# Attention loads as casting transfers on one queue, and output copies on two engines

## The chip, the cores and the metric

The kernel runs on one core of one Trainium2 chip. The metric is the time of one execution in device microseconds (us); medians of several executions are quoted, and profiles show one execution each. The span of a profile is about 2 us shorter than the time of the same execution. Engines are named as the profile names them: PE (matrix engine), PEld (its weight loads), DVE (VectorE), ACT (ScalarE), POOL (GpSimd) and SP (SyncE, which here only issues transfers).

## The reference

A decayed linear attention over 4 batches, 8 heads, 768 positions and 64 channels, followed by an expert layer with an ELU between its two products. In the kernel's terms, for chunks of 128 positions:

```python
# attention, per head, chunks of 128 (the reference uses 64; the result is the same)
out_chunk = (q k^T * decay_mask) v + (q * lam_pow) state
state     = lam_block * state + (k * rev_pow)^T v
# expert layer, x is [3072, 512]
h = x @ w_in                                  # 512 -> 2048
g = where(h > 0, h, exp(min(h, 0)) - 1)
y = g @ w_out                                 # 2048 -> 512
```

All inputs are fp32; the kernel computes in fp16 with fp32 accumulators.

## The kernel before

There are 24 chunks of attention (g = 0 to 23) and 8 token tiles of the expert layer (m = 0 to 7), three chunks to a tile. Chunks 0 to 2 are computed in a prologue. From then on one loop of 128 slots runs the expert layer, 16 slots to a tile, and the attention of the next tile is spread over the slots of this one by the function F. The parts that matter (cut):

```python
# the six chunks of batch 0: raw fp32 loads from SP, cast later on ACT and DVE
lam_p = ...                               # two loads of 64 x 4 values, every second one of lam
for c in range(NCB):
    for dst, src in zip(raw0, (q, k, v)):
        nc.sync.dma_start(out=dst[:, c], in_=src[0, :, c*L:(c+1)*L].rearrange("h p d -> p h d"))

def emit_w_load(i):                       # weights: casting loads from POOL
    nc.gpsimd.dma_start(out=wi16[i][:], in_=moe_w_in[:, f0:f1]...)
    nc.gpsimd.dma_start(out=wo16[i][:], in_=moe_w_out[f0:f1, :]...)

def att_ev(g):                            # transposed q and k out of PSUM
    nc.scalar.copy(out=qt[:], in_=pt[:, 0])
    nc.scalar.copy(out=z[0:64, :, 0, :], in_=pt[0:64, 1])
    nc.scalar.copy(out=z[64:128, :, 1, :], in_=pt[64:128, 1])

def att_SU(g, hp):                        # scores and state update of one head pair
    pu = ps.tile([128, 512], FP32, tag="psSU")       # ONE buffer
    ...three matmuls into pu...
    nc.vector.tensor_tensor(out=P[:], in0=pu[:, 0:256]..., in1=mask[...], op=ALU.mult)
    ...two state updates on nc.vector from pu...

def att_PI(g, hp):
    if hp == 0: psO[g] = ps.tile([128, NHP, 128], FP32, tag="psO")   # ONE buffer
    ...
def att_X(g):                             # frees psO
    nc.vector.tensor_tensor(out=xt[...], in0=psO.pop(g)[:], in1=qs[:], op=ALU.mult)

# at the end of a tile (its last slot but for a lag of 2)
for i in range(CPT):
    nc.vector.tensor_copy(o[:], psM[m][i][:])
    nc.sync.dma_start(out=out[t0:t0+128, :], in_=o[:])

def F(g):                                 # first slot of chunk g
    t, c = divmod(g, CPT)
    if t == 1: return 3 + 3*c
    return (t - 1)*NFT - 2 + 5*c
# T at F; SU of head pair hp at F+2+hp; PI at F+3+hp; X at F+6
```

## Time and profile before

Median 270.64 us (270.54 to 271.5) when it was predicted.

| what | before |
|---|---|
| first expert matmul (psH) starts | 31.42 us |
| from there to the end of the first tile | 47.00 us |
| later tiles, alternating | 27.94 and 27.60 us |
| last raw load used | 60.12 us |

A tile's end is read here as the start of the first psM_2 matmul of the next tile: by then all three accumulators have been copied out and PE has restarted. Those times are 35.59, 78.42, 106.36, 133.96, 161.90, 189.50, 217.44 and 243.84.

First, lines of the page of the kernel before: the span, PE's busy share, then the busy tenths of PE and of the transfer engines (DMA) in 40 slices of 6.7 us each, and the shares of the chain of work that ended last.

```profile
span 268.1 us, 4675 instructions
PE 224.0 (84%) x1632; PEld 134.2 (50%) x1632; DVE 192.2 (72%) x461; ACT 159.8 (60%) x351; POOL 73.4 (27%) x111
...
PE   0166678585989998999899989999899989998991
...
DMA  0999999999998479567956894793300030003003
...
PE 63%; SPq 15%; DVE 8%; DMA 7%; issue 4%; ACT 1%; DVEq 0%; ACTq 0%
```

PE's row stays at 8 or less through slice 10 (67 us), and its 9s follow one another only from slice 13 (80 us) on. The DMA row is at 9, its highest digit, from slice 2 to slice 12: transfers are under way all through the start. SPq in the chain is SP's issuing.

The table of stretches of the kernel before (busy us and instructions of each engine, granted clock, DMA share, rate):

```profile
core 0: us, PE busy (x) PEld busy (x) DVE busy (x) ACT busy (x) POOL busy (x), PEclk, DMA share, GB/s
20.00:30.00 10.00, 6.44 (x51) 5.37 (x52) 9.50 (x27) 2.28 (x5) 5.05 (x7) 1.00 1.48 175
...
80.00:100.00 20.00, 20.00 (x157) 12.30 (x155) 17.96 (x45) 14.54 (x33) 8.65 (x11) 1.00 0.68 47
```

From 20 to 30 us DVE is busy 9.50 of 10 us: it paces the prologue. From 80 us PE is busy throughout. (The DMA share in this view adds up the recorded times of all packets over 16 engines; above 1, as in 1.48, it means that packets overlapped on an engine.)

The timeline of the kernel before (start us, duration us, engine, line, operation, out<-in; in brackets idle time just before and what ended it):

```profile
1.24 1.36 SPq L64 DMA_DIRECT2D lam_p<-in_lam_dram  x2
...
3.92 4.70 SPq L74 DMA_DIRECT2D raw_v<-in_v_dram  x1
...
31.42 1.44 PE L312 MATMUL psH_381<-xt_265,wi_0_104 128*128 128x384 f16 x4 [0.78 <-DVE xt_265 L298]
...
60.12 0.43 DVE L190 CAST v_5_153<-raw_v 128x512 f16<-128x512 f32 x1 [2.45 <-DMA raw_v<-in_v_dram]
...
104.42 0.69 DVE L345 COPY osb_0_1308<-psM_0_909 128x512 f32<-128x512 f32 x1
105.03 0.68 DVE L345 COPY osb_1_1311<-psM_1_910 128x512 f32<-128x512 f32 x1
...
105.16 0.38 PE L338 MATMUL psM_0_1345<-wo_0_109,g_1277 128*128 128x512 f16 x1 [0.86 <-DVE osb_0_1308 L345]
105.62 0.68 DVE L345 COPY osb_2_1314<-psM_2_911 128x512 f32<-128x512 f32 x1
...
105.76 0.38 PE L338 MATMUL psM_1_1346<-wo_0_109,g_1277 128*128 128x512 f16 x1 [0.22 <-DVE osb_1_1311 L345]
...
106.36 0.38 PE L338 MATMUL psM_2_1347<-wo_0_109,g_1277 128*128 128x512 f16 x1 [0.22 <-DVE osb_2_1314 L345]
```

The third raw load's issue keeps SP for 4.70 us. The last raw_v is cast at 60.12, and DVE waited 2.45 us for it. At the tile end (104 to 107 us) three DVE copies run one after the other, 0.60 apart, and each restart of PE waits for one of them.

### The profile page before, as it was taken

To read this page: it belongs to the slowest core of one execution; us is meant where nothing else is said; L and a number is where in the kernel's file an instruction comes from. 1 tells how busy PE (TensorE), PEld (TensorE's weight loads), DVE (VectorE), ACT (ScalarE), POOL (GpSimd) and SP (SyncE) were. 2 spreads that over 40 slices of the span, in tenths; PEclk is the share of its full clock that TensorE was granted. 3 is DMA by queue.
4 is the path that set the end of the run, shared out by engine and by line. 5 is a ranking of instruction groups with operands and counts; after the bars stand their busy time and mean duration, and the time that the engine had idled before them with its cause. 6 is when DMAs were issued, how large, how long until landed. Compare 5 with 4: busy or idle time off the path is not lost.

```text
span 268.1 us, 4675 instructions
## 1 busy us (share of the span) xinstructions
PE 224.0 (84%) x1632; PEld 134.2 (50%) x1632; DVE 192.2 (72%) x461; ACT 159.8 (60%) x351; POOL 73.4 (27%) x111
## 2 busy tenths in 40 slices
PE   0166678585989998999899989999899989998991
PEld 0045434243555664666466655665466546553550
DVE  1259646437699979977789979867999799655443
ACT  2673078362647764776577576757666756764660
POOL 8195414225524430433242333232000000000000
PEclk9999999889999999999999999999999999999999
DMA  0999999999998479567956894793300030003003
GB/s 1 205 210 183 174 180 177 196 176 111 63 172 55 31 49 118 77 43 48 86 111 44 57 59 129 50 60 22 119 2 0 0 120 0 2 0 120 0 2 119
DMA packets 84104, 22.60 MB, mean 84 GB/s; under 512 B 76400, under 2 KB 81008, under 8 KB 84080
## 3 DMA queue, kind: packets, MB, share of 16 engines
q0 software_dynamic: 61216, 11.28, 51.1%
q1 hardware_dynamic: 22864, 11.02, 17.6%
q8 instruction: 13, 0.21, 0.3%
q14 instruction: 11, 0.09, 0.1%
HBM read 27.27 MB, written 6.29 MB: 125 GB/s over the span
## 4 chain that ended last, share of the span: by engine, by line
PE 63%; SPq 15%; DVE 8%; DMA 7%; issue 4%; ACT 1%; DVEq 0%; ACTq 0%
SPq L74 14%; DMA raw_v<-in_v_dram 7%; PE psM_2_2205 L338 1%; PE psM_2_3057 L338 1%; PE psM_2_2627 L338 1%; PE psM_2_1769 L338 1%; PE psM_2_911 L338 1%; PE psM_2_1347 L338 1%; PE psM_0_1767 L338 1%; PE psM_0_1345 L338 1%; PE psM_0_2625 L338 1%; PE psM_0_2203 L338 1%; PE psM_0_909 L338 1%; PE psM_1_1346 L338 1%; PE psM_1_2204 L338 1%
## 5 line engine op out<-in xcount | busy, mean ns | idle before, releaser
L312 PEld LDWEIGHTS <-wi_3_107 128*128 128x128 f16 x128 | 12.7, 100 | 14.5 <-DMA wi_3_107<-in_moe_w_in_dram 2.5
L312 PEld LDWEIGHTS <-wi_2_106 128*128 128x128 f16 x128 | 12.5, 98 | 11.7
L312 PEld LDWEIGHTS <-wi_4_108 128*128 128x128 f16 x128 | 12.5, 98 | 11.7
L218 PE MATMUL psT_187<-ident_118,qn_182 128*128 128x128 f16 x4 | 0.6, 308 | 12.6 <-ACT qn_182 L188 12.6
L312 PEld LDWEIGHTS <-wi_1_105 128*128 128x128 f16 x64 | 6.4, 100 | 8.9 <-issue 4.2
L242 PEld LDWEIGHTS <-kz_154 128*128 128x128 f16 x96 | 8.3, 105 | 4.9 <-POOL kd_200 L201 1.5
L181 POOL DMA_DIRECT2D v_3_151<-in_v_dram x6 | 4.5, 753 | 22.4 <-PE psO_2149 L289 8.7
L312 PEld LDWEIGHTS <-wi_0_104 128*128 128x128 f16 x64 | 6.5, 103 | 7.5 <-issue 2.0
L242 PEld LDWEIGHTS <-kz_155 128*128 128x128 f16 x96 | 8.0, 101 | 3.5 <-issue 1.4
L181 POOL DMA_DIRECT2D v_0_148<-in_v_dram x6 | 4.5, 757 | 15.6 <-PE psO_1715 L282 8.4
L181 POOL DMA_DIRECT2D v_1_149<-in_v_dram x6 | 4.5, 750 | 13.5 <-PE psO_1003 L289 5.0
L181 POOL DMA_DIRECT2D v_4_152<-in_v_dram x6 | 4.5, 755 | 12.4 <-PE psO_1441 L289 5.0
L181 POOL DMA_DIRECT2D v_5_153<-in_v_dram x6 | 4.5, 756 | 11.7 <-PE psO_2431 L289 4.3
L181 POOL DMA_DIRECT2D v_2_150<-in_v_dram x6 | 4.5, 757 | 9.3 <-PE psO_1140 L289 4.6
L141 DVE TENSOR_TENSOR mask<-causT,dn 128x1024 f32<-128x1024 f32 x1 | 1.2, 1224 | 7.8 <-ACT dn L130 7.8
L218 PEld LDWEIGHTS <-qn_182 128*128 128x128 f16 x4 | 0.3, 130 | 12.6 <-ACT qn_182 L188 12.6
L317 ACT ACTIVATE e_386<-psH_381 128x384 f32<-128x384 f32 x1 | 0.5, 492 | 8.6 <-PE psH_381 L312 8.6
L282 PEld LDWEIGHTS <-v_2_150 128*128 128x128 f16 x32 | 3.4, 106 | 3.4 <-issue 1.9
L282 PEld LDWEIGHTS <-v_4_152 128*128 128x128 f16 x32 | 3.2, 99 | 3.7 <-issue 1.8
L282 PEld LDWEIGHTS <-v_1_149 128*128 128x128 f16 x32 | 3.4, 108 | 2.6 <-issue 1.0
L282 PEld LDWEIGHTS <-v_5_153 128*128 128x128 f16 x32 | 3.1, 98 | 2.8 <-issue 0.9
L282 PEld LDWEIGHTS <-v_0_148 128*128 128x128 f16 x32 | 3.2, 108 | 2.3 <-issue 0.6
(1917 smaller groups left out, 863.6 us busy)
## 6 DMA issues: line engine op xcount, KB each, us to landing
raw_q<-in_q_dram SPq DMA_DIRECT2D x6, 256.0 KB, 8.8
raw_k<-in_k_dram SPq DMA_DIRECT2D x6, 256.0 KB, 9.7
raw_v<-in_v_dram SPq DMA_DIRECT2D x6, 256.0 KB, 10.0
wi_2_106<-in_moe_w_in_dram POOLq DMA_DIRECT2D x1, 512.0 KB, 15.4
wo_2_111<-in_moe_w_out_dram POOLq DMA_DIRECT2D x1, 512.0 KB, 17.7
wi_3_107<-in_moe_w_in_dram POOLq DMA_DIRECT2D x1, 512.0 KB, 17.6
wo_3_112<-in_moe_w_out_dram POOLq DMA_DIRECT2D x1, 512.0 KB, 20.2
wi_4_108<-in_moe_w_in_dram POOLq DMA_DIRECT2D x1, 512.0 KB, 19.8
```

The source lines that it names most:

```text
L74: nc.sync.dma_start(out=dst[:, c], in_=src[0, :, c * L : (c + 1) * L].rearrange("h p d -> p h d"),)
L141: nc.vector.tensor_tensor(out=mask[:], in0=causT[:].unsqueeze(1).broadcast_to([128, H, 128]), in1=dn[:].unsqueeze(2).broadcast_to([128, H, ...
L181: nc.gpsimd.dma_start(out=vz[:, :, 2 * hh, :], in_=v[b, hh::2, rows].rearrange("h p d -> p h d"))
L218: nc.tensor.transpose(pt[:, 0, hp, :], in_=qn[:, 2 * hp : 2 * hp + 2, :], identity=ident16[:])
L242: nc.tensor.matmul(pu[:, hh * 128 : (hh + 1) * 128], lhsT=z[:, hp, hh, :], rhs=qt[:, hp, :], start=True, stop=True,)
L282: nc.tensor.matmul(po[:, hp, :], lhsT=vz[:, hp, hh : hh + 2, :], rhs=P[:, hh, :], start=(hh == 0), stop=(hh == 1 and cb == 0), skip_group_ ...
L312: nc.tensor.matmul(pH[:], lhsT=wi[:, kk, j * 128 : (j + 1) * 128], rhs=xt[m][:, kk, :], start=(kk == 0), stop=(kk == NHP - 1),)
L317: nc.scalar.activation(e[:], pH[:], AF.Exp)
L338: nc.tensor.matmul(psM[m][i][:], lhsT=g[:, i * 128 : (i + 1) * 128], rhs=wo16[wof[n][0]][:, wof[n][1], :], start=(n == 0), stop=(n == NFT ...
```

## The change

Its intent: load every chunk's q, k and v with casting transfers from POOL, all on one queue with the weights and in the order of need; lay v out with a zero block beside every head, so that one load fills it; and share the copying of outputs between DVE and ACT. Cut to its core:

```diff
-    lam_p = ...two loads of every second lam...
-    raw0 = [...fp32 tiles...]; for c in range(NCB): ...nc.sync.dma_start(raw...)...
+    v2 = [cpool.tile([128, 2 * H, 64], FP16, ...) for i in range(NB)]
+    def emit_load(g, which=(0, 1, 2)):
+        jobs = ((qn[:], q), (kn[:], k), (vz[:, 0::2, :], v))
+        for dst, src in [jobs[i] for i in which]:
+            nc.gpsimd.dma_start(out=dst, in_=src[b, :, rows].rearrange("h p d -> p h d"))
+    emit_load(0, (0, 1))
...
-    nc.scalar.activation(loglam_p[:], lam_p[:], AF.Ln)
+    for hh in range(2): nc.vector.tensor_copy(loglam_p[r, :], loglam[r, hh::2])
...
+    emit_load(0, (2,)); emit_load(1); emit_load(2)
...
-        nc.gpsimd.memset(...)      # zeros in kz, v3 and st: 18 memsets
+        nc.vector.memset(...)      # the same for kz, v2 and st, after the mask
...
-        nc.scalar.copy(out=qt[:], in_=pt[:, 0])
+        if g < CPT: nc.vector.tensor_copy(qt[:], pt[:, 0])
+        else:       nc.scalar.copy(out=qt[:], in_=pt[:, 0])
...
-                    nc.vector.tensor_copy(new[r, r], u)     # state of a first chunk
+                    nc.scalar.copy(new[r, r], u)
...
-                nc.vector.tensor_copy(o[:], psM[m][i][:])
+                if i == 1: nc.vector.tensor_copy(o[:], psM[m][i][:])
+                else:      nc.scalar.copy(o[:], psM[m][i][:])
...
+    emit_w_load(0); emit_w_load(1); emit_load(3); emit_w_load(2); emit_load(4)
+    emit_w_load(3); emit_load(5); emit_w_load(4)
```

More of the change, by code (lines that the diff above doesn't have):

```diff
@@ L51 @@
     wpool = ctx.enter_context(tc.tile_pool(name="w", bufs=1))
-    raw = ctx.enter_context(tc.tile_pool(name="raw", bufs=1))
     nat = ctx.enter_context(tc.tile_pool(name="nat", bufs=6))
@@ L60 @@
     nc.sync.dma_start(out=lam_b[:], in_=lam.unsqueeze(0).broadcast_to([128, H]))
-    lam_p = cpool.tile([128, NHP], FP32, name="lam_p")
-    for hh in range(2):
-        nc.sync.dma_start(
-            out=lam_p[hh * 64 : (hh + 1) * 64, :],
-            in_=lam[hh::2].unsqueeze(0).broadcast_to([64, NHP]),
-        )
-    raw0 = [
-        raw.tile([128, NCB, H, 64], FP32, name=f"raw_{n}", tag=f"raw_{n}") for n in "qkv"
-    ]
-    for c in range(NCB):
-        for dst, src in zip(raw0, (q, k, v)):
-            nc.sync.dma_start(
-                out=dst[:, c],
-                in_=src[0, :, c * L : (c + 1) * L].rearrange("h p d -> p h d"),
-            )
+    NB = 6
+    v2 = [cpool.tile([128, 2 * H, 64], FP16, name=f"v2_{i}") for i in range(NB)]
+    nats = {}
+    def emit_load(g, which=(0, 1, 2)):
+        b, c = divmod(g, NCB)
+        rows = slice(c * L, (c + 1) * L)
+        if 0 in which:
+            qn = nat.tile([128, H, 64], FP16, tag="qn", name=f"qn{g}")
+            kn = nat.tile([128, H, 64], FP16, tag="kn", name=f"kn{g}")
+            nats[g] = (qn, kn, v2[g % NB])
+        qn, kn, vz = nats[g]
+        jobs = ((qn[:], q), (kn[:], k), (vz[:, 0::2, :], v))
+        for dst, src in [jobs[i] for i in which]:
+            nc.gpsimd.dma_start(out=dst, in_=src[b, :, rows].rearrange("h p d -> p h d"))
+    emit_load(0, (0, 1))
     WG = [2, 2, 4, 4, 4]
@@ L104 @@
     loglam_p = cpool.tile([128, NHP], FP32, name="loglam_p")
-    nc.scalar.activation(loglam_p[:], lam_p[:], AF.Ln)
+    for hh in range(2):
+        r = slice(hh * 64, (hh + 1) * 64)
+        nc.vector.tensor_copy(loglam_p[r, :], loglam[r, hh::2])
     ident16 = cpool.tile([128, 128], FP16, name="ident16")
@@ L122 @@
     nc.gpsimd.iota(iota_r[:], pattern=[[1, 128]], base=0, channel_multiplier=0)
+    emit_load(0, (2,))
+    emit_load(1)
+    emit_load(2)
     pos = cpool.tile([128, 2], FP32, name="pos")
@@ L146 @@
     )
-    NB = 6
-    v3 = [cpool.tile([128, NHP, 3, 64], FP16, name=f"v3_{i}") for i in range(NB)]
     kz = [cpool.tile([128, NHP, 2, 128], FP16, name=f"kz_{i}") for i in range(2)]
@@ L156 @@
     for i in range(2):
-        nc.gpsimd.memset(kz[i][64:128, :, 0, :], 0.0)
-        nc.gpsimd.memset(kz[i][0:64, :, 1, :], 0.0)
+        nc.vector.memset(kz[i][64:128, :, 0, :], 0.0)
+        nc.vector.memset(kz[i][0:64, :, 1, :], 0.0)
     for i in range(NB):
-        nc.gpsimd.memset(v3[i][:, :, 1, :], 0.0)
+        nc.vector.memset(v2[i][:, 1::2, :], 0.0)
     for hp in range(NHP):
         for i in range(2):
-            nc.gpsimd.memset(st[hp][i][:], 0.0)
-    nats = {}
-    def nat_tiles(g):
-        qn = nat.tile([128, H, 64], FP16, tag="qn", name=f"qn{g}")
-        kn = nat.tile([128, H, 64], FP16, tag="kn", name=f"kn{g}")
-        nats[g] = (qn, kn, v3[g % NB])
-        return nats[g]
-    def emit_load(g):
-        b, c = divmod(g, NCB)
-        qn, kn, vz = nat_tiles(g)
-        rows = slice(c * L, (c + 1) * L)
-        nc.gpsimd.dma_start(out=qn[:], in_=q[b, :, rows].rearrange("h p d -> p h d"))
-        nc.gpsimd.dma_start(out=kn[:], in_=k[b, :, rows].rearrange("h p d -> p h d"))
-        for hh in range(2):
-            nc.gpsimd.dma_start(
-                out=vz[:, :, 2 * hh, :], in_=v[b, hh::2, rows].rearrange("h p d -> p h d")
-            )
-    def emit_cast_first(c):
-        qf, kf, vf = raw0
-        qn, kn, vz = nat_tiles(c)
-        nc.scalar.copy(qn[:], qf[:, c])
-        nc.scalar.copy(kn[:], kf[:, c])
-        nc.vector.tensor_copy(
-            vz[:, :, 0::2, :], vf[:, c].rearrange("p (g t) d -> p g t d", t=2)
-        )
+            nc.vector.memset(st[hp][i][:], 0.0)
     kds = {}
@@ L199, in att_kd @@
         kd = asb.tile([128, H, 64], FP16, tag="kd", name=f"kd{g}", bufs=2)
-        eng = nc.gpsimd if g == 0 else nc.vector
-        eng.tensor_tensor(
+        nc.vector.tensor_tensor(
             out=kd[:], in0=nats[g][1][:],
@@ L229, in att_ev @@
         z = kz[g % 2]
-        nc.scalar.copy(out=qt[:], in_=pt[:, 0])
-        nc.scalar.copy(out=z[0:64, :, 0, :], in_=pt[0:64, 1])
-        nc.scalar.copy(out=z[64:128, :, 1, :], in_=pt[64:128, 1])
+        if g < CPT:
+            nc.vector.tensor_copy(qt[:], pt[:, 0])
+        else:
+            nc.scalar.copy(out=qt[:], in_=pt[:, 0])
+        for hh in range(2):
+            r = slice(hh * 64, (hh + 1) * 64)
+            nc.scalar.copy(out=z[r, :, hh, :], in_=pt[r, 1])
         qT[g] = (qt, z)
@@ L250, in att_SU @@
                 lhsT=kds[g][:, 2 * hp : 2 * hp + 2, :],
-                rhs=vz[:, hp, 0::2, :], start=True, stop=True,
+                rhs=vz[:, 4 * hp : 4 * hp + 3 : 2, :], start=True, stop=True,
             )
@@ L283, in att_PI @@
                 po[:, hp, :],
-                lhsT=vz[:, hp, hh : hh + 2, :],
+                lhsT=vz[:, 4 * hp + hh : 4 * hp + hh + 2, :],
                 rhs=P[:, hh, :], start=(hh == 0), stop=(hh == 1 and cb == 0),
@@ L344, in mm2 @@
                 o = msb.tile([128, DM], FP32, tag="osb", bufs=4, name=f"osb{m}_{i}")
-                nc.vector.tensor_copy(o[:], psM[m][i][:])
+                if i == 1:
+                    nc.vector.tensor_copy(o[:], psM[m][i][:])
+                else:
+                    nc.scalar.copy(o[:], psM[m][i][:])
                 t0 = m * MT + i * 128
@@ L364 @@
         f = F(g)
-        evs.append((f, lambda g=g: (emit_cast_first(g) if g < NCB else None, att_T(g), att_ev(g), att_kd(g))))
+        evs.append((f, lambda g=g: (att_T(g), att_ev(g), att_kd(g))))
         for hp in range(NHP):
@@ L372 @@
         at(s, fn)
-    loads = [(-1, lambda: emit_w_load(0)), (-1, lambda: emit_w_load(1))]
-    loads += [(4 * i - 4, lambda i=i: emit_w_load(i)) for i in range(2, len(WG))]
-    for g in range(NCB, NG):
-        loads.append((F(g) - 12, lambda g=g: emit_load(g)))
-    loads.sort(key=lambda x: x[0])
-    for g in range(CPT):
-        emit_cast_first(g)
-        if g == 1:
-            loads.pop(0)[1]()
-        if g == 2:
-            loads.pop(0)[1]()
+    emit_w_load(0)
+    emit_w_load(1)
+    emit_load(3)
+    emit_w_load(2)
+    emit_load(4)
+    emit_w_load(3)
+    emit_load(5)
+    emit_w_load(4)
+    loads = [(F(g) - 12, lambda g=g: emit_load(g)) for g in range(NCB, NG)]
+    for g in range(CPT):
         att_T(g)
```

## The prediction

> **What bounds the kernel now.**
>
> 1. Prologue, 0 to 31.4 us: PE idles; the first expert matmul (psH_381) starts at 31.42 (timeline). VectorE paces it: in 20 to 30 us it is busy 9.50 of 10 us (windows table).
> 2. First token tile, 31 to 78 us: loads. The chain of waits runs through SyncE's load issues (14%) and raw_v's DMA (7%). In the trace's packet records for 48 to 54 us the two queues advance one for one: about 310 weight packets (1024 B) and 312 raw packets (256 B) per 2 us. The Trainium skill, "DMA: Bandwidth & Descriptors", section Queues, rings and completion order, says each engine alternates between queues packet by packet; the trace agrees. So small raw loads move at the pace of large weight packets, 40 GB/s, and the last raw_v lands at 60.1. The first tile's closing-to-closing time (psM_2's restart, 35.59 to 78.42) is 42.8 us; later tiles take 27.54 to 27.94 (mean 27.80).
> 3. Steady state, 80 to 262 us: PE, chain of waits nearly all psH matmuls. By the pure-matmul slot time of 1.297 us a tile would need about 25.8; the other 2 us sit mostly at the tile end, where PE waits for three serial VectorE copies (osb, spaced 0.60): at 104.1 to 106.57 it loses about 1.8 us.
>
> **What changes, with costs.**
> - Removed: 12 ScalarE casts (0.62 each), 6 VectorE casts (0.43 to 0.77), the 256-byte queue, and the lam_p load, whose landing at 8.77 held up the exponentials (near 5 after).
> - Moved to VectorE, before its first attention work: 18 memsets, v's zeros doubled. The skill, "VectorE: DVE Perf Modes", section Zero memsets, gives one cycle per element; my estimate from it is 0.55 for 512 elements, about 6.5 us in all. No trace shows one yet: my largest unknown. Also three qT copies (estimate 0.5) and kd(0) (0.68).
> - One queue, in order. Between 60 and 62 us casting loads alone moved 1216 packets per us, so a 1024-packet load needs 0.84 us of transfer and about 0.9 of POOL issue; the nine first loads land by about 13 us (landing 3.7 to 3.9 after issue). Weights (4.2 MB written, 155 GB/s) and the next nine loads then land by about 45, ahead of use in every slot.
> - Steady state: two of three osb copies and each first chunk's state copies go to ScalarE; VectorE drops to about 22.5 us per tile.
>
> **Critical path.** VectorE free at about 13, then about 15 us of the three prologue chunks: first expert matmul at 27.5 (gain 4). First tile: 42.8 to about 30 (gain 13; attention is denser there and VectorE may bind). Six later boundaries: gain 1.2 each, period about 26.5 (gain 7). Final copies: gain 0.6. Sum about 25 us of 270.64.
>
> **Prediction: 245.5 us, 80% range 240 to 252. Chances: faster by over 2% 0.97, within 2% 0.02, slower 0.01.**
>
> **Signs.** First psH matmul at 25 to 30 us; no PE wait on a DMA after it; no second cold-clock stretch (now 52.2 to 55.6); psM_2 restarts 26 to 27 us apart; last weight landed before 48 us; VectorE memsets 5 to 7 us in all.
>
> **What would make it wrong.** Memsets costing 2 us or 10; POOL's issue slowed while VectorE works, so chunks 1 and 2 come late; the first tile's dense attention making VectorE bind, keeping it at 33 or more; ScalarE's copies delaying the exponentials and moving the boundary bubble rather than filling it.

## More of the kernel before

The eight PSUM banks are all in use: psT, psSU and psO have one each, psM three, psH two.

## The result and the profile after

Median 250.68 us (250.40 to 250.93, 4 runs) against 270.86 us (270.54 to 271.5, 4 runs) for the kernel before in the same rounds. Ratio 0.9252, 95% interval 0.9231 to 0.9273. A ratio is the mean time of one kernel's runs over that of the other's of the same rounds, so it is not quite the ratio of the medians quoted.

The page of the changed kernel, the same lines (slices of 6.2 us):

```profile
span 248.7 us, 4595 instructions
PE 220.5 (89%) x1632; PEld 133.8 (54%) x1632; DVE 178.7 (72%) x431; ACT 164.7 (66%) x383; POOL 72.1 (29%) x92
...
PE   0186797869999989999999989999999999999991
...
DMA  6999999999995596499589769563000020003003
...
PE 66%; DMA 8%; ACT 8%; DVE 7%; issue 4%; POOL 4%; ACTq 0%; DVEq 0%; POOLq 0%
```

PE's 9s follow one another from slice 10 (56 us) on, in place of 80 us. The DMA row is again at 9 from slice 2 to slice 12: the transfers are as busy as before, yet they stop PE far less. SPq is gone from the chain.

The stretches of the changed kernel:

```profile
core 0: us, PE busy (x) PEld busy (x) DVE busy (x) ACT busy (x) POOL busy (x), PEclk, DMA share, GB/s
...
40.00:58.00 18.00, 13.98 (x124) 9.05 (x123) 12.96 (x34) 9.07 (x21) 10.85 (x13) 1.00 2.07 151
...
80.00:100.00 20.00, 19.35 (x153) 11.84 (x151) 17.33 (x44) 13.91 (x33) 5.26 (x6) 1.00 0.83 86
```

Between 40 and 58 us PE is busy 13.98 of 18 us. Something in the first tile still stops it; the experiments show what.

The start of the changed kernel in the timeline:

```profile
7.62 0.27 DVE L162 MEMSET kz_143<- 64x256 uint32 x1
...
11.11 0.11 DVE L168 MEMSET st_1_152<- 128x64 uint32 x1
11.14 0.35 DVE L207 COPY qT_205<-psT_196 128x512 f16<-128x512 f16 x1
...
11.53 1.19 ACT L212 COPY kz_143<-psT_196 64x512 f16<-64x512 f16 x2 [3.82 <-DVE qT_205 L207]
...
21.00 0.42 DVE L207 COPY qT_310<-psT_301 128x512 f16<-128x512 f16 x1
...
21.52 1.19 ACT L212 COPY kz_143<-psT_301 64x512 f16<-64x512 f16 x2 [4.82 <-DVE qT_310 L207]
...
27.78 1.44 PE L292 MATMUL psH_376<-xt_267,wi_0_87 128*128 128x384 f16 x4 [0.78 <-DMA wo_2_94<-in_moe_w_out_dram]
```

The memsets run from 7.62 to 11.2 us, just before the first qT copy on DVE. ACT's kz copy begins only when DVE's qT copy has ended, after 3.82 and 4.82 us of idling. The first psH matmul starts at 27.78. Its bracket names a load of wo_2, a tile that this matmul does not read; DVE's xt_267, which it reads, ended at 27.73. The label is of the kind that is looked at under c_space4.

Where the 19.4 us of the two spans (268.1 and 248.7) came from. Each row is a difference of two times in the timelines.

| stage | before | after | gain | gain predicted |
|---|---|---|---|---|
| start to first expert matmul | 31.42 | 27.78 | 3.6 | 3.9 |
| from there to the end of the first tile | 47.00 | 37.08 | 9.9 | 13 |
| the six tiles after it | 165.42 | 159.94 | 5.5 | 7 |
| the last tile and the final copies | 24.26 | 23.90 | 0.4 | 0.6 |

The gains came in the stages predicted, but the sum was 5 us too large, most of it in the first tile. The prediction gave the delay of that tile one reason, the loads, and named its dense attention only as a risk.

### The profile page after: what moved, and what is told of

Read it like the earlier page. It is cut to its first block, busy times and chain, and to the rows that moved or that the text cites. A ratio compares the mean times of both kernels' runs of the same rounds, so it can differ in the third digit from the quotient of the medians.

```text
span 248.7 us, 4595 instructions
## 1 busy us (share of the span) xinstructions
PE 220.5 (89%) x1632; PEld 133.8 (54%) x1632; DVE 178.7 (72%) x431; ACT 164.7 (66%) x383; POOL 72.1 (29%) x92
## 4 chain that ended last, share of the span: by engine, by line
PE 66%; DMA 8%; ACT 8%; DVE 7%; issue 4%; POOL 4%; ACTq 0%; DVEq 0%; POOLq 0%
DMA wo_2_94<-in_moe_w_out_dram 4%; DMA wi_0_87<-in_moe_w_in_dram 3%; PE psM_1_2165 L318 1%; PE psM_1_1313 L318 1%; ACT kz_144 L212 1%; PE psM_2_2166 L318 1%; PE psM_2_1314 L318 1%; PE psM_1_3012 L318 1%; PE psM_0_1312 L318 1%; PE psM_2_3013 L318 1%; PE psM_0_2164 L318 1%; DMA kn_991<-in_k_dram 1%; PE psM_0_3011 L318 1%; PE psM_0_3371 L318 1%; PE psM_0_879 L318 1%
## 5 line engine op out<-in xcount | busy, mean ns | idle before, releaser
L77 POOL DMA_DIRECT2D v_3_80<-in_v_dram x4 | 3.6, 906 | 16.2 <-PE psO_1259 L269 8.1
L77 POOL DMA_DIRECT2D v_0_77<-in_v_dram x4 | 3.5, 880 | 15.8 <-PE psO_1680 L262 7.7
L77 POOL DMA_DIRECT2D v_5_82<-in_v_dram x4 | 3.5, 878 | 15.3 <-PE psO_2391 L269 5.0
L77 POOL DMA_DIRECT2D v_4_81<-in_v_dram x4 | 3.5, 878 | 13.1 <-PE psO_2260 L269 5.6
L77 POOL DMA_DIRECT2D v_1_78<-in_v_dram x4 | 3.6, 889 | 11.6 <-PE psO_1825 L269 5.9
L77 POOL DMA_DIRECT2D v_2_79<-in_v_dram x4 | 3.6, 896 | 10.7 <-PE psT_2046 L198 5.5
L222 PE MATMUL psSU_0_211<-qT_205,kz_143 128*128 128x128 f16 x2 | 0.6, 288 | 5.5 <-ACT kz_143 L212 5.5
L194 PE MATMUL psT_196<-ident_102,qn_83 128*128 128x128 f16 x4 | 0.6, 308 | 4.8 <-DMA qn_83<-in_q_dram 4.8
L212 ACT COPY kz_143<-psT_301 64x512 f16<-64x512 f16 x2 | 1.2, 580 | 4.8 <-DVE qT_310 L207 4.8
```

The lines of the kernel that those rows point to most:

```text
L77: nc.gpsimd.dma_start(out=dst, in_=src[b, :, rows].rearrange("h p d -> p h d"))
L194: nc.tensor.transpose(pt[:, 0, hp, :], in_=qn[:, 2 * hp : 2 * hp + 2, :], identity=ident16[:])
L212: nc.scalar.copy(out=z[r, :, hh, :], in_=pt[r, 1])
L222: nc.tensor.matmul(pu[:, hh * 128 : (hh + 1) * 128], lhsT=z[:, hp, hh, :], rhs=qt[:, hp, :], start=True, stop=True,)
```

## The experiments

Twelve kernels ran, all correct. "Start" is the first psH matmul; "first tile" goes from there to the tile's end. This second number varies by up to 1 us between traces of kernels that do not differ there, and most of that is the moment at which the matrix clock rises, since the first slots run at half clock. (The Trainium skill, "TensorE: Matmul & The Clock Gate", section What's actually happening, has PE start at half clock and rise after about 3.4 us of work, and calls the moment variable. The traces agree roughly: in the changed kernel the grant is full from 31.9 us, 4.1 us after the start; over all runs this took 2.6 to 6.0 us.) Medians of different rounds are compared with care: the kernel before itself took 270.86 to 272.11 us in them, and j_late_loads, whose edit turned out to move nothing, lies 0.8 us below the changed kernel. Differences of about 1 us in the median are therefore read from the traces, not from the medians.

| kernel | start | first tile | later periods | median us | ratio |
|---|---|---|---|---|---|
| before | 31.42 | 47.00 | 27.94 / 27.60 | 270.86 | 1 |
| changed | 27.78 | 37.08 | 27.39 / 26.17 | 250.68 | 0.9252 |
| a_osb_dve | 27.57 | 37.31 | 28.36 / 27.06 | 256.82 | 0.9455 |
| b_evac_only | 32.47 | 44.71 | 27.41 / 26.17 | 264.57 | 0.9727 |
| c_space4 | 27.66 | 32.80 | 27.39 / 26.17 | 245.96 | 0.9054 |
| h_osb_act | 27.67 | 37.84 | 26.62 / 26.66 | 249.56 | 0.9179 |
| d_memset_first | 24.27 | 37.94 | 27.39 / 26.17 | 247.13 | 0.9084 |
| e_no_lam_p | 29.25 | 42.88 | 27.94 / 27.60 | 263.58 | 0.9696 |
| f_small_w | 31.51 | 44.85 | 27.94 / 27.60 | 266.81 | 0.9821 |
| j_late_loads | 27.78 | 36.79 | 27.38 / 26.17 | 249.89 | 0.9197 |
| g_qT_act | 26.27 | 38.01 | 27.39 / 26.17 | 249.48 | 0.9187 |
| k_evac_no_lam_p | 30.51 | 41.05 | 27.40 / 26.16 | 257.37 | 0.9488 |
| i_comb2 | 24.32 | 32.85 | 26.62 / 26.16 | 240.42 | 0.8854 |
| l_comb3 | 23.55 | 32.71 | 26.62 / 26.17 | 239.49 | 0.8821 |

### Undo the evacuation (a_osb_dve), and do it alone (b_evac_only)

```diff
 # a_osb_dve, on the changed kernel
-                if i == 1: nc.vector.tensor_copy(...)
-                else:      nc.scalar.copy(...)
+                nc.vector.tensor_copy(o[:], psM[m][i][:])
 # b_evac_only, on the kernel before
+                if i == 1: nc.vector.tensor_copy(...) else: nc.scalar.copy(...)
-                    nc.vector.tensor_copy(new[r, r], u)
+                    nc.scalar.copy(new[r, r], u)
```

> The changed kernel with all three output copies of a tile put back on VectorE (the state copies of first chunks stay on ScalarE). My theory: the tile-end wait of PE for three serial VectorE copies (0.60 apart) returns in full; tile periods go from 27.39/26.17 back to about 27.8/27.4, over seven tile ends, and the whole to 255 to 258 us. Rival: the shorter periods come from VectorE's relief over the whole tile (fewer copies, no load casts), not from the wait at the tile end; then putting 1.2 us per tile back on VectorE, which has about 4 us of room per tile, costs under 2 us and the whole stays below 252.5.

> The kernel before with only the evacuation part of the change: output copies 0 and 2 and the state copies of first chunks on ScalarE, loads untouched. If the two parts act in different stages, this gains about what the tile ends are worth, 5 to 6 us: 264 to 266 us, with the first tile still at 42 to 43 us between restarts of psM_2 and later periods of 26 to 27.4. If the parts depend on each other (the evacuation only helps once the loads no longer stall PE), it gains under 2 us.

Undone, the kernel takes 256.82 us, 6.1 more, and every period grows by 0.9 to 1.0. Done alone on the kernel before, it gains about 7.3 us and gives the same periods as the whole change, 27.41 and 26.17. So the later periods belong to this part alone, and it does not need the loads' part. Two details were not expected. Alone, it also shortened the first tile by 2.3 us. And the start came 1.05 us later: there the state copies of chunk 0 were the only part of the edit that ran before the first expert matmul. In its trace ACT's first cast for chunk 1 comes at 18.41 in place of 15.47, behind eight state copies that begin at 16.65, and PE waits 2.02 us for it.

### Chunks four slots apart in the first tile (c_space4), and later loads (j_late_loads)

What stops PE between 40 and 58 us of the changed kernel? The chain of waits gives this answer (start us, duration us, what):

```profile
50.62 3.24 DMA kn_991<-in_k_dram
53.85 0.27 PE psO_706 L262 x2
```

The timeline around that moment, and around two more stops:

```profile
43.37 0.27 PE L222 MATMUL psSU_0_576<-qT_515,kz_143 128*128 128x128 f16 x2 [1.27 <-DVE st_0_151 L248]
...
45.27 0.69 DVE L278 TENSOR_TENSOR xt_601<-psO_494,qs 128x512 f16<-128x512 f32 x1
...
46.02 0.27 PE L262 MATMUL psO_603<-pp_0_580,v_4_81 128*128 128x128 f16 x2 [0.86 <-DVE xt_601 L278]
...
50.62 0.88 POOL L77 DMA_DIRECT2D kn_991<-in_k_dram  x1
...
53.11 0.69 DVE L278 TENSOR_TENSOR xt_601<-psO_603,qs 128x512 f16<-128x512 f32 x1 [0.57 <-PE psO_603 L269]
...
53.85 0.27 PE L262 MATMUL psO_706<-pp_0_681,v_5_82 128*128 128x128 f16 x2 [0.78 <-DMA kn_991<-in_k_dram]
```

The load of kn_991 was issued at 50.62 and belongs to a chunk that is not computed for many slots. The instruction that it is said to release, psO_706, writes a buffer that DVE's xt_601 had to read out first, and xt_601 ran from 53.11 to 53.80. The label is wrong; which event a wait belongs to is inferred by time. The other brackets name the same kind of release: psSU waits for DVE's last read of it (st, 1.27 us), psO for xt (0.86 us).

The kernel before has the same stops in its first tile, 1.11 and 1.29 us for psSU and twice 0.78 for psO, among its waits for loads and casts. The first of them:

```profile
52.10 0.35 PE L242 MATMUL psSU_0_597<-qT_533,kz_154 128*128 128x128 f16 x2 [1.11 <-DVE st_0_162 L268]
```

These stops come from the schedule. A chunk needs SU at slots F+2 to F+5, PI at F+3 to F+6 and X at F+6. In the first tile chunks start three slots apart, so the next chunk's first SU falls in the same slot as this one's last, and its first PI in the same slot as this one's X. Both pairs share a single PSUM buffer, so PE stands still until DVE has worked off its queue. Later tiles use five slots and never meet.

```diff
 # c_space4, on the changed kernel
         if t == 1:
-            return 3 + 3 * c
+            return 1 + 4 * c
 # j_late_loads, on the changed kernel
-    loads = [(F(g) - 12, lambda g=g: emit_load(g)) for g in range(NCB, NG)]
+    loads = [(F(g) - 6, lambda g=g: emit_load(g)) for g in range(NCB, NG)]
```

> The changed kernel with one number changed: the chunks of the first tile's attention stage start at slots 1, 5, 9 in place of 3, 6, 9. My theory: the first tile takes 32.7 us in place of 26 to 27.4 because with three slots between chunks two chunks meet in one slot, and share single PSUM buffers: PE waits 1.27 and 1.10 us for psSU, and 0.86 and 0.78 for psO, with VectorE's queue behind it. With four slots between they never meet: first tile 28 to 30 us, the whole 246.5 to 248.5. Rival, which the chain of waits names: PE waits there for the transfer of k (3.24 us put down to a load of kn): then bringing chunks 3 and 4 forward helps nothing, and the whole stays at 250.7 or gets longer.

> The changed kernel with the loads of chunks 6 and later issued 6 slots ahead of use in place of 12. The chain of waits puts 3.24 us of the first tile down to a load of kn (chunk 8 or 9), at a time when the DMA engines move loads that nobody needs for many slots. My theory: that is a mislabel (the real release is VectorE's xt copy), so taking these loads out of 44 to 54 us changes nothing: 250.7 within 0.5. Rival: the loads' traffic does hold up the first tile: 1.5 to 3 us faster.

With four slots between chunks the kernel takes 245.96 us, 4.7 less and a little better than expected, and the first tile loses 4.3 us. The time from restart to restart is then 27.63, close to that of later tiles, and of the waits for psSU and psO in that tile 0.18 us is left. The stretch in which PE was busy 13.98 of 18 us:

```profile
core 0: us, PE busy (x) PEld busy (x) DVE busy (x) ACT busy (x) POOL busy (x), PEclk, DMA share, GB/s
40.00:58.00 18.00, 17.68 (x144) 10.86 (x142) 14.52 (x34) 12.42 (x29) 12.70 (x15) 1.00 2.21 157
```

PE is now busy 17.68 of 18, with the transfers just as busy (DMA share 2.21 here, 2.07 before the edit). That answers the rival: the same traffic, and PE hardly waits.

j_late_loads was meant to answer it too, but its edit did not do what the text above says. The same row of its trace:

```profile
40.00:58.00 18.00, 13.99 (x122) 8.91 (x120) 12.95 (x33) 9.08 (x21) 10.10 (x12) 1.00 2.10 152
```

The loads are still there. Chunk 6's first load was issued at 41.68 us in place of 42.46, and between 44 and 54 us 155 GB/s moved in both kernels. POOL's program has nothing but loads at this point, so the slot in which one is emitted does not hold it back; it is issued as soon as POOL gets to it and its buffers are free. The first tile stayed as it was (32.67 from restart to restart, 32.68 without the edit), which says nothing about the traffic. The total, 249.89 us, is 0.8 below the changed kernel, outside the 0.5 expected, and shows how far medians of different rounds differ when nothing has changed.

So the spacing was the cause and the transfers were not. That the single buffers are the way in which the spacing acts is read from the waits; no run gave psSU or psO a second buffer.

### All output copies on ACT (h_osb_act)

The tile end that costs most in the changed kernel, in its timeline:

```profile
89.85 0.59 ACT L328 COPY osb_0_1276<-psM_0_879 128x512 f32<-128x512 f32 x1
...
90.32 0.62 ACT L328 COPY osb_2_1282<-psM_2_881 128x512 f32<-128x512 f32 x1
...
91.01 0.38 PE L318 MATMUL psM_0_1312<-wo_0_92,g_1245 128*128 128x512 f16 x1
...
91.29 0.69 DVE L326 COPY osb_1_1279<-psM_1_880 128x512 f32<-128x512 f32 x1
...
92.03 0.38 PE L318 MATMUL psM_1_1313<-wo_0_92,g_1245 128*128 128x512 f16 x1 [0.65 <-DVE osb_1_1279 L326]
...
92.25 0.38 PE L318 MATMUL psM_2_1314<-wo_0_92,g_1245 128*128 128x512 f16 x1
```

ACT's two copies are done by 90.9, but the middle one waits in DVE's queue until 91.29, so psM_1 restarts at 92.03, 0.65 us late.

```diff
-                if i == 1: nc.vector.tensor_copy(...)
-                else:      nc.scalar.copy(...)
+                nc.scalar.copy(o[:], psM[m][i][:])
```

> The changed kernel with all three output copies of a tile on ScalarE. My theory: what is left of the bubble (PE waits about 0.65 to 0.8 us for the middle copy, which stands behind VectorE's backlog at every second tile end) goes, periods become 26.1 to 26.5 throughout, the whole 247 to 249. Rival: three ScalarE copies in a row (1.7 us) hold up the next exponentials and the bubble moves there: no gain, 250 to 252.

The periods became flat, 26.62 and 26.66; the total fell by about 1 us only. At the odd tile ends, where DVE has a backlog, three ACT copies are better by 0.77 us. At the even ones, where DVE is free, they are worse by 0.49. In the timeline of this kernel, at an even tile end, the next exponential stands behind the three copies:

```profile
117.17 1.56 ACT L325 COPY osb<-psM 128x512 f32<-128x512 f32 x3
...
117.81 1.35 PE L318 MATMUL psM<-wo,g 128*128 128x512 f16 x3
...
118.61 0.52 ACT L297 ACTIVATE e<-psH 128x384 f32<-128x384 f32 x1
```

PE's three restarts spread over 1.35 us here, where those of the odd end before it took 0.84, and the exponential starts 1.44 us after the first copy, where it takes 0.96 at the same end of the changed kernel. Both theories were half right: the total (249.56 us) lies between their ranges. The best version below uses each form where it is better.

### The memsets first (d_memset_first)

```diff
     v2 = [cpool.tile(...)]
+    kz = ...; st = ...          # tiles and all 18 nc.vector.memset(...) moved here,
                                 # ahead of DVE's first other work
```

> The changed kernel with VectorE's 18 memsets moved to the head of its program, where it idles for its first 3.6 us. My theory: the memsets (7.62 to 11.14 us, 3.5 us in all) stand on the critical path between the mask and the first chunk's qT copy; moved, the first expert matmul starts 2.5 to 3.2 us earlier (24.6 to 25.3 in place of 27.79) and the whole is 247.4 to 248.4. Rival: the loads of chunks 1 and 2 (landing about 11 and 13.6 us) or the first tile's wait for weights pace the start: gain under 1 us, or given back in the first tile.

The first expert matmul came at 24.27, 3.5 us earlier, and the kernel took 247.13 us, 3.55 less; both are slightly better than expected. (The span of the profiled execution gained only 2.7; its clock rose 5.9 us after the start in place of 4.1.) The 18 memsets were practically wholly on the critical path, though they need no input and DVE was idle for the first 3.6 us. They cost 3.6 us in all, not the 6.5 of the prediction. The Trainium skill, "VectorE: DVE Perf Modes", section Zero memsets, gives one cycle per element, and also says that a zero memset can be issued over 4-byte words, halving the elements of fp16. The trace shows that this was done: 256 uint32 elements for 512 fp16 ones, 0.27 us each. The prediction used the rule and overlooked the second half of it.

### The qT copies back on ACT (g_qT_act)

ACT's kz copies and DVE's qT copy only read the same psT tile, yet one engine waits for the other. The Trainium skill, "PSUM — Partial Sum Buffer", section Terms, lists two engines on one bank and partition group at once as an error, "reads against reads included". That is a reason for such a wait, which therefore can't simply be dropped; no run here shows the error.

```diff
-        if g < CPT: nc.vector.tensor_copy(qt[:], pt[:, 0])
-        else:       nc.scalar.copy(out=qt[:], in_=pt[:, 0])
+        nc.scalar.copy(out=qt[:], in_=pt[:, 0])
```

> The changed kernel with the first three chunks' qT copies put back on ScalarE. In the changed kernel ScalarE's kz copies begin only after VectorE's qT copy of the same psT tile has ended, and so stand behind VectorE's queue (3.82 us of ScalarE idling in chunk 0, 4.82 in chunk 2), while VectorE then waits 1.11, 0.54 and 0.43 us for the products that need kz. Theory: the move of qT to VectorE cost more than it saved; undone, the first expert matmul starts 0.8 to 1.8 us earlier (26.0 to 27.0) and the whole is 249.0 to 250.0. Rival: ScalarE needs 0.5 us more per chunk in series, and the start stays at 27.8 or gets later.

The start came at 26.27, 1.5 us earlier, within the range expected. In the timeline ACT's copies of chunk 0 now run while DVE still fills zeros (kz at 8.09 in place of 11.53):

```profile
7.63 0.56 ACT L206 COPY qT<-psT 128x512 f16<-128x512 f16 x1
...
8.09 1.18 ACT L209 COPY kz<-psT 64x512 f16<-64x512 f16 x2
```

So moving qT to DVE was a loss as the change stands. Little of the gain can be seen in the total: 249.48 us, 1.2 less. The interval of its ratio (0.9160 to 0.9215) lies just below that of the changed kernel (0.9231 to 0.9273), but inside that of j_late_loads (0.9151 to 0.9243), which does the same work as the changed kernel. In its trace the first tile is 0.9 us longer: full clock came 6.0 us after the start, in place of 4.1.

### The kernel before without lam_p (e_no_lam_p)

```diff
-    lam_p = cpool.tile([128, NHP], FP32, name="lam_p")
-    for hh in range(2): nc.sync.dma_start(out=lam_p[...], in_=lam[hh::2]...)
-    nc.scalar.activation(loglam_p[:], lam_p[:], AF.Ln)
+    for hh in range(2): nc.vector.tensor_copy(loglam_p[r, :], loglam[r, hh::2])
```

> The kernel before without the two small lam_p loads (4-byte pieces, first in the loading queue); the same values are copied from lam_b, as the change does. My theory: prologue starts earlier (the raw loads' packets begin near 3 us in place of 6.7, the exponentials near 5 in place of 9) and the first expert matmul comes 2 to 4 us sooner, but the last raw_v still lands near 57 to 60 us, since the shared queues pace it, so most of the gain is given back in the first tile: 267.5 to 270.5 us. Rival: the start is worth its full 3 us to the end: 267.5 or less.

It gained 7.7 us (263.58 against 271.24). The theory's range was missed; the rival's (267.5 or less) holds, but for more than its reason: the start moved only 2.2 us. The issues of SP in this kernel's timeline, to be set beside those of the kernel before:

```profile
1.24 0.42 SPq L68 DMA_DIRECT2D raw_q<-in_q_dram  x1
...
2.33 1.30 SPq L68 DMA_DIRECT2D raw_v<-in_v_dram  x1
...
3.67 0.89 SPq L68 DMA_DIRECT2D raw_q<-in_q_dram  x1
```

SP is no longer held for 4.70 us, and the packet records agree. Counted there:

| | before | without lam_p |
|---|---|---|
| 4-byte packets on SP's queue up to 9.2 us | 581 | 99 |
| first 256-byte raw packet | 7.10 us | 2.32 us |
| raw packets begun by 10 us | 2334 | 6348 |
| first weight packet | 16.1 us | 14.5 us |
| last raw packet | 59.6 us | 48.0 us |

Two loads of 1 KB each, cut into 4-byte pieces, stood ahead of the raw loads and held them up by 4.8 us. The Trainium skill, "DMA: Bandwidth & Descriptors", section Rules for kernel authors, says that a strided last dimension lowers to one descriptor per element; the traces agree: SP's queue moved 544 fewer 4-byte packets in all (688 in place of 1232) for two loads of 512 values together. Why was the gain larger than the 2.2 us at the start? Until weights join in, the raw loads have the transfer engines to themselves and move at 214 to 239 GB/s (counted in steps of 2 us). Afterwards they share, and in the kernel before they move at 33 to 111. So 4.8 us more of undisturbed time brought the last raw packet forward by 11.6 us, and the first tile, which waits for it, lost 4.1 us.

### Small weight packets in the kernel before (f_small_w)

```diff
-        nc.gpsimd.dma_start(out=wi16[i][:], in_=moe_w_in[:, f0:f1]...)
-        nc.gpsimd.dma_start(out=wo16[i][:], in_=moe_w_out[f0:f1, :]...)
+        for j in range(WG[i]):   # blocks of 128 columns
+            nc.gpsimd.dma_start(out=wi16[i][:, :, j*128:(j+1)*128], in_=...)
+        for j in range(4):
+            nc.gpsimd.dma_start(out=wo16[i][:, :, j*128:(j+1)*128], in_=...)
```

> The kernel before with each weight load cut into column blocks of 128, so that its packets write 256 B in place of 1024 (or 512); same bytes, same order, more packets and more issues on POOL. My theory of the first tile before: the two queues advance one packet each in turn, so the 256-byte raw packets move at 40 GB/s only because each waits for a 1024-byte weight packet. Then raw packets in the shared stretch advance at 80 GB/s or more, the last raw_v lands before 50 us in place of 60.1, and the first tile shortens by 4 us or more (unless late weights take its place). Rival: the raw loads are held by the sheer number of packets or bytes, or by SyncE's issue: then more packets make it worse, and the last raw_v lands at 60 or later.

With weight packets of 256 bytes the raw loads moved at 85 to 130 GB/s between 32 and 40 us, where those of the kernel before had 39 to 46 between 44 and 54 us beside 1024-byte packets. The last raw packet landed at 45.1 in place of 59.6, though nothing was changed about the raw loads. That fits the alternation of the skill's section Queues, rings and completion order, which the prediction rests on. The counts are about one for one here too: 3344 raw and 2957 weight packets from 32 to 40 us. (The page's packet holds several descriptors; whether a turn is one of the trace's packets or several, the counts don't tell.) The kernel gained 4.4 us, with an interval of 1.3% to 2.3%, though the weights, now slower, arrived until 61.2 us (59.5 before). One part of the expectation failed: the first tile was to lose 4 us or more and lost 2.1 (44.85 in place of 47.00), although the last raw load came 14.5 us earlier. Late weights took little of it back (PE waited 0.34 us for one); the clock, full 5.8 us after the start in place of 3.7, took an estimated 1 us. So the slow raw loads were only a part of what made the old first tile long; the stops at psSU and psO are in this trace as well (1.11, 0.86, 1.11 and 0.78 us).

### The two small parts together (k_evac_no_lam_p)

The edits of b_evac_only and e_no_lam_p together on the kernel before.

> The kernel before with two small parts of the change and none of its casting loads: no lam_p loads, and the evacuation on two engines. If the two single gains (7.7 and 7.3 us) lie in different stages they add: 255.5 to 257 us; what the casting loads on one queue are worth beyond that is then the rest to 250.7, about 5 to 6 us, a quarter of the whole gain. If they overlap in the first tile (both shortened it), 258 or more.

257.37 us, 14.1 less than the kernel before (271.51): nearly the sum of 7.3 and 7.7, a little outside the range expected. So about 70% of the change's 20.2 us come from not loading lam_p by elements and from the output and state copies. All the rest, casting loads on one queue and the moves that go with them, is worth about 6.5 us: 2.7 at the start (30.51 against 27.78) and 4.0 in the first tile (41.05 against 37.08). No run separates the parts of this rest.

### Everything that helped (i_comb2, l_comb3)

```diff
 # i_comb2 on the changed kernel: c_space4, d_memset_first, g_qT_act, and
-                if i == 1:
+                if i == 1 and m % 2 == 0:
                     nc.vector.tensor_copy(o[:], psM[m][i][:])
 # l_comb3 on i_comb2: qT of chunks 0 and 1 back on DVE
+        if g < 2: nc.vector.tensor_copy(qt[:], pt[:, 0])
+        else:     nc.scalar.copy(out=qt[:], in_=pt[:, 0])
```

> Everything that helped, together: chunk spacing 4 in the first tile, VectorE's memsets at its head, qT of the first chunks on ScalarE, and the middle output copy on ScalarE too at every second tile end (the odd tiles, where VectorE has a backlog). If the gains lie in different stages they add: 4.7 + 3.5 + 2.2 + 1.3 off 250.7, 238.5 to 240.5 us; first expert matmul at 22.5 to 23.5, first tile 26.5 to 28, later periods 26.1 to 26.7 throughout. Rival: the earlier start runs into the loads of chunks 1 to 3 or the first weights, and 2 us or more are given back: 241.5 or more.

> The best version so far (240.42 us) with the qT copies of chunks 0 and 1 back on VectorE and only chunk 2's on ScalarE. Moving the memsets alone gave a first expert matmul at 24.27, and qT on ScalarE added nothing to it (24.32), though alone it was worth 1.5 us. My reading: with the memsets gone VectorE is the freer engine in chunks 0 and 1 (it waits 1.64 and 1.02 us there for products that need ScalarE's kz), and only in chunk 2, where ScalarE idles 2.36 us, is qT better on ScalarE. Then the first expert matmul comes at 23.4 to 24.0 and the whole is 239.4 to 240.2. Rival: the start is now set by VectorE's total work whatever engine copies qT; then 24.3 to 24.8 and 240.4 or more.

i_comb2 took 240.42 us. The gains of the first tile and of the tile ends added; those at the start did not. The memsets alone gave 24.27, with qT on ACT as well 24.32. Both edits attacked the same wait: once DVE was free early, ACT became the engine that chunks 0 and 1 waited for. l_comb3 follows from that and copies qT on the freer engine in each chunk; its start is 23.55, and its time 239.49 us, ratio 0.8821 (0.8791 to 0.8850). It is the best version, 4.5% below the changed kernel.

## Why the prediction was right, and where its sizes were off

- **The range and the direction.** 250.68 us lies inside 240 to 252, near its upper end. The estimate of 245.5 was 5.2 us too low.
- **The prologue (27.5 predicted, 27.78 measured) was right by two errors that cancelled.** The memsets were priced at 6.5 us and took 3.6. The three chunks after DVE became free were given about 15 us and took 16.6 (11.14 to 27.78); the wait of ACT's kz copies for DVE's qT copies was worth 1.5 us of it. The prediction priced qT on DVE as DVE work and missed that it also held up ACT. d_memset_first and g_qT_act show both parts.
- **The first tile (42.8 to about 30 predicted, from restart to restart; 32.68 measured) is the largest mis-sized term.** The prediction named one cause of the old delay, raw loads that share with large weight packets, and f_small_w shows that sharing; but it also shows that this cause alone was worth only 2 to 3 us of the first tile, and not doing lam_p's loads was worth 4.1. The prediction allowed about 2 us for dense attention making DVE bind. The real remainder over a normal tile was about 5 us, and came from two chunks meeting in a slot with one psSU and one psO buffer; c_space4 takes it away whole. The same stops are in the trace of the kernel before, among its waits for loads. DVE was busy 12.96 of the 18 us from 40 to 58, and 14.52 in c_space4 without the stops: the amount of its work did not bind, as the prediction feared.
- **The tile ends (1.2 us each predicted).** (Its 27.54 for the shortest old period should be 27.60.) Even ones gained 1.4, odd ones 0.55. At the odd ones the middle copy stayed behind DVE's backlog. Among the reasons to be wrong the prediction named ACT's copies delaying exponentials; that was not it in the changed kernel, and appeared only with all three copies on ACT.
- **lam_p was named, for the wrong thing.** The prediction counted its removal because its landing at 8.77 us held up the exponentials. Its main cost was the 4.8 us by which it delayed every raw load.
- **The signs.** The start, the last weight (44.4 us), no second cold stretch and no true wait of PE for a load after the start were as written (the one wait so labelled, 0.78 us for kn_991, is DVE's xt). The spacing of restarts (26.17, but also 27.39) and the memsets' 5 to 7 us were not.

What stays open: that the evacuation alone delays the start by 1.05 us through chunk 0's state copies on ACT is read from its trace; no run undid that part alone. The 0.9 us by which the first tile is longer in d_memset_first and g_qT_act than in the changed kernel fits the clock: it rose 1.8 and 1.9 us later after the start, and at half clock that is an estimated 0.9 us of work; no run tests it apart. Why the rise came when it did was not looked into.

## What to carry to other kernels

Order small loads by what stands behind them: two loads of 1 KB in 4-byte pieces cost 7.7 us here, because they stood first in their queue and the time that they took was the only time in which the loads behind them were undisturbed. When a wait has been removed, look at the same stretch again before giving the credit for all of it: here about 5 us of stops at shared buffers lay beside the loads, and one number in the schedule took them away. After an edit, look in the trace whether it moved what it was meant to move: j_late_loads did not, and its unchanged time would have been taken for proof. Before moving a copy from one engine to another, check who else reads the same PSUM tile and which engine is idle at that very moment; the better choice differed between chunks and between odd and even tiles.

## What the Trainium skill lacked or had wrong

- "DMA: Bandwidth & Descriptors" has no rates for casting loads. Here a single casting queue wrote 148 to 155 GB/s (reading twice that) with 128-byte packets and 202 to 207 GB/s with 1024-byte packets.
- The same page has the turns by packet, but not what follows for a queue of small packets beside one of large ones: 256-byte raw packets moved at 39 to 46 GB/s beside 1024-byte packets and at 85 to 130 beside 256-byte ones.
- It also gives no size for what element-wise loads do to loads behind them: about 480 packets of 4 bytes delayed the next load's first packet from 2.32 to 7.10 us.
- "VectorE: DVE Perf Modes" says that a zero memset can be issued as uint32, not that it is done unasked; here it was, 0.27 us for 512 fp16 zeros.
- "PSUM — Partial Sum Buffer" says that two engines must not read one bank at once, but puts no cost on it. Here ACT idled 3.8 and 4.8 us until a DVE copy of the other half of the same tile had ended; DVE had other work before that copy.
- No page read warns that a wait can be credited to a load that merely was issued near it: 3.24 us were, in the chain of waits of the changed kernel, and 10.39 us before its first expert matmul (to a load of wo_2, which that matmul does not read).
